# Attention into two layered products on one core: the softmax sums divided earlier, a start in written order, a new order of the parts, and six more filled slots

## The chip, the cores and the metric

The kernel runs on one core of one Trainium2 chip. The metric is device time in microseconds (us), the median of three runs. The core has a TensorE (PE) for products, VectorE (DVE), ScalarE (ACT) and GpSimd (POOL) for the rest, and SyncE (SP), whose queue issues all transfers of this kernel. PEld is the load of weights into TensorE.

## The reference

q, k and v have 4 batches, 8 heads, 576 rows and 64 columns, f one value per row; all is float32 (weights are handed to the kernel as float64 words).

```
scores = q k^T / 8 ;  cum = cumsum(log(clip(f, 1e-4, 1)))
scores = where(causal, scores + cum_i - cum_j, -1e9)
attn   = exp(scores - rowmax);  attn = attn / (rowsum(attn) + 1e-9)
x = attn v               -> 2304 x 512
h = x w_in               -> 2304 x 2048;  g = h tanh(log(1 + e^h)) (Mish);  y = g w_out   -> 2304 x 512
ab = (y w1) * (y w2)     -> 2304 x 1024;  out = (ab w3) w_out2                            -> 2304 x 512
```

## The kernel before

**Two phases.** Phase A has the attention, the conversion of the float64 words of all weights, the product w3 w_out2 ("wp"), and as much of the first layer as is ready. Phase B has the rest of the first layer and then two halves ("quads") of the later layers. A float32 operand stands as a high and a low part, and one product is three passes (high high, high low, low high). In phase B seven products of half matrices stand for eight; they are numbered 1 to 7, and the letter o is that number.

**Slots.** The 32 heads go in 16 pairs, each pair in four slots (64, and four for what is left). Slot j of a pair has the scores of query blocks c = (0, 1), (2, 3), (4) for j = 0, 1, 2 (`score`, L711), the product with v of the pair before at j = 3 (`pv`), and the transposes of the probabilities of the slot before (`turn`, L700). Between them stand products from a list, the filler: 192 of wp in slots 0 to 20, then products of the first layer, 24 in each of the slots 21 to 36, 12 in each of 37 to 52, none in 53 to 63, and 24 in each of 64 and 65 (`plan`, L592). A unit of the first layer is 12 products into one bank, and its copy h goes to DRAM (L554 to L562). Units that are left run in phase B behind the attention (`cover`); there they are 144 products.

**Softmax.** `softmax` takes scores plus mask out of PSUM with a running minimum (VectorE, L390, L396, L397), then exponentials on ScalarE with their row sums (L400). The probabilities stay undivided. At slot 3 of a pair the nine columns of sums get a reciprocal (`inv_sums`, L403), are transposed with the identity (L705), copied (L416), stored in DRAM (L417) and loaded back as a tile R, one row for all partitions of a head (`inv_load`, L419). `x_rows` multiplies the product with v by R (L482).

**The start.** `decay_log` computes log f on 128 partitions of 144 values. `decay_rows` gathers them on 32 partitions of 576 by four transfers (L279), scans them, makes high and low parts of both signs, and loads rows of these into the score operands `aug` (L344 to L348); a copy goes to DRAM for later pairs. Ten weight tiles (two of w3, eight of w_out2) are converted by an exponent pass on ScalarE (L134), three passes on VectorE (L142 to L144), a cast on ScalarE (L99) and a subtraction on GpSimd (L113).

**What sets the order.** TensorE runs in written order. The other engines are ordered at build time by a scheduler from priorities (`high_priority`) and from its own estimate; `issue_after` (`behind`, `between`) keeps an instruction behind another one of its engine.

**The first layer in phase B.** Eight m, seven parts each, 12 products a part, 56 steps. The order is that of `m_order` (L801): 5, 6, 2, 3, 7, then part 1 of the next m, then part 4. Parts 6, 7 and 4 add into the bank of part 1, and the addition to 7 (L1057) must have read that bank before 4 writes it; 5 and 3 share one bank. A hook behind each part puts in `s_sums` and `s_build` for the next m, the conversion of w1 and w2, and at the end `k_begin`, the operands of the next layer. The gate layers use the same `m_layer` and order.

Of the kernel before, what the change touches and what calls it, by code (L numbers as in the profile page):

```python
# [34 lines left out]
LAST = 2 * S - 64  # L35

# [6 lines left out]
NEAR = 2  # L43
MID = 7
EARLY = 10
# [31 lines left out]
class Kernel:  # L77
# [18 lines left out]
    def split(self, raw, hi, lo, hi_eng="act", lo_eng="dve"):  # L96
        nc = self.nc
        if hi_eng == "act":
            nc.scalar.copy(hi, raw)  # L99
# [17 lines left out]
    def cv_load(self, key, src, where=None):  # L117
# [5 lines left out]
        self.nc.sync.dma_start(dst, src)  # L123
# [12 lines left out]
    def cv_bits(self, key):  # L136
# [7 lines left out]
        dve.scalar_tensor_tensor(ti, w[:, :, 0], 29, ti, ALU.logical_shift_right, ALU.bitwise_or)  # L144

    def cv_split(self, key, hi, lo, hi_eng="act", lo_eng="pool"):
        self.split(self.cv.pop(key)[1], hi, lo, hi_eng, lo_eng)
        self.fresh.add(key)
# [45 lines left out]
    def pools(self):  # L194
# [7 lines left out]
        self.inv_scr = d.tile([NPAIR, 9, 128], F32, name="inv_scr")  # L202
# [14 lines left out]
    def att_pool(self):  # L217
# [12 lines left out]
        self.ident = a.tile([128, 128], F32, name="ident")  # L230
        self.m1 = a.tile([128, 512], BF16, name="m1")
# [39 lines left out]
    def decay_rows(self, between, after):  # L271

        nc, dve = self.nc, self.nc.vector
        lf = self.att.tile([128, S], F32, name="lf", tag="xx", bufs=1)
        cum = self.att.tile([128, S], F32, name="cum", tag="R", bufs=1)
        for i in range(4):
            ins = nc.sync.dma_start(lf[0:32, 144 * i:144 * i + 144], self.lf[32 * i:32 * i + 32])  # L279
        with self.tc.issue_after(ins.ins):  # L280
            between()
        dve.tensor_tensor_scan(cum[:32], lf[:32], lf[:32], 0.0, ALU.add, ALU.bypass)
        slot = self.pt[0:32, 3].bitcast(F32R)
        ch, cl, nh, nl = [slot[:, i] for i in range(4)]
        dve.tensor_scalar(ch, cum[:32], 8.0, None, ALU.mult)
        nc.scalar.mul(nh, f32(ch), -1.0)
        dve.scalar_tensor_tensor(cl, cum[:32], 8.0, f32(ch), ALU.mult, ALU.subtract)
        dve.tensor_scalar(nl, f32(cl), -1.0, None, ALU.mult)
        cs = self.cum_scr.rearrange("(p t) r c -> t p r c", t=2)
        q, k = f32(slot[:, 0:2]), f32(slot[:, 2:4])  # L290
        self.cum_sb = (q, k)
        self.load_cum(0)
        ins = self.load_cum(1)
        nc.sync.dma_start(cs[0, :, 0:2], q[0:16])
        nc.sync.dma_start(cs[0, :, 2:4], k[0:16])
        nc.sync.dma_start(cs[1, :, 2:4], k[16:32])
        nc.sync.dma_start(cs[1, :, 0:2], q[16:32])
        with self.tc.issue_after(ins.ins):
            after()


    def consts(self):
        nc = self.nc
        make_identity(nc, self.ident)
        nc.gpsimd.memset(self.m1, 0.0)
# [33 lines left out]
    def load_cum(self, h):  # L339
        nc = self.nc  # L340
        t = f32(self.aug[h // 2 % 2])
        r = 64 * (h % 2)
        q, k = (self.cum_scr[h, 0:2], self.cum_scr[h, 2:4]) if h > 1 else [x[16 * h:16 * h + 1] for x in self.cum_sb]
        nc.sync.dma_start(t[r + 2:r + 4, 0:S], k)  # L344
        if h % 2 == 0:
            return nc.sync.dma_start(t[r:r + 2, S:2 * S], q)
        nc.sync.dma_start(t[r:r + 2, 2 * S:KQ], q[..., 512:])
        return nc.sync.dma_start(t[r:r + 2, S:LAST], q[..., :512])  # L348

# [26 lines left out]
    def softmax(self, p, c):  # L376
# [7 lines left out]
        if c < 4:  # L384
# [7 lines left out]
            cols = (c, 5 + c)  # L392
        else:
# [4 lines left out]
            cols = (4,)  # L398
# [4 lines left out]
    def inv_sums(self):  # L403

        nc = self.nc
        r = self.sums[:, 0:9]
        nc.scalar.activation(r, r, AF.Copy, bias=1e-9)
        nc.vector.reciprocal(r, r)
        self.inv = r

    def inv_rows(self, p):

        nc = self.nc
        t = self.att.tile([16, 128], F32, name=f"inv{p}", tag="inv", bufs=1)
        with self.tc.high_priority(offset=HP_SM):
            nc.scalar.copy(t[0:9], self.ps_t[1][0:9, 384:512])  # L416
        nc.sync.dma_start(self.inv_scr[p], t[0:9])  # L417

    def inv_load(self, p):  # L419
        self.R = self.att.tile([128, S], F32, name=f"R{p}", tag="R", bufs=1)  # L420
        d = self.inv_scr[p:p + 1].rearrange("o i q -> o (i q)")
        self.nc.sync.dma_start(self.R[0:64], d[:, :S].broadcast_to([64, S]))
        self.nc.sync.dma_start(self.R[64:128, :512], d[:, 640:].broadcast_to([64, 512]))
        self.nc.sync.dma_start(self.R[64:128, 512:], d[:, S:640].broadcast_to([64, 64]))
# [51 lines left out]
    def x_rows(self, p):  # L476
# [5 lines left out]
        self.nc.vector.tensor_tensor(x, self.ps_v[:, 256:832], self.R, ALU.mult)  # L482
# [59 lines left out]
    def l1_unit(self, b, m, half):  # L542
# [4 lines left out]
        def step(c, k, i):  # L547
# [46 lines left out]
    def plan(self):  # L594
# [8 lines left out]
        cnt += [24] * (L1_S[1] - WP_END) + [12] * 16 + [0] * (NU * NPAIR - L1_S[1] - 16)  # L603
        return cnt + [24, 24] + [0] * NU

    def phase_a(self):
# [12 lines left out]
        self.decay_log()  # L619
        self.load_raw(0)  # L620
        self.consts()
        self.zeros()

# [4 lines left out]
        def after():  # L628
# [677 lines left out]
```

## Time and profile before

| | us |
|---|---|
| median of 3 runs | 958.28 (957.95 to 958.51) |
| the profiled execution | 958.19 |
| its span | 956.4 |
| mean granted TensorE clock | 0.980 |
| TensorE busy | 883.2 (92%) |
| VectorE busy | 687.5 (72%) |
| ScalarE busy | 496.3 (52%) |
| GpSimd busy | 203.4 (21%) |

The span is from the first to the last instruction, and what lies around it is 1.8 us. Busy shares are averages over stages with different limits. A wait is put down to what ended last before it. In the busy table by stretches, PEclk is the granted TensorE clock as a share of full speed.

### The profile page before, as it was taken

Reading aid. Unit: us, or ns where it says so; the run is one execution under the profiler, and the core shown is the slowest. Engines: PE = TensorE matmul, PEld = TensorE weight load, DVE = VectorE, ACT = ScalarE, POOL = GpSimd, SP = SyncE. Lnnn points to the kernel's source line nnn. Section 1 sums busy time; section 2 is a strip of 40 time slices with the busy share of each in tenths; the row PEclk is TensorE's granted clock in tenths of the full one; section 3 lists DMA queues with packets and bytes.
Section 4 is the critical chain, followed back from the end, with each engine's and each line's share of the span. In section 5 each row is a group of like instructions: output and inputs, shape, how many; then the busy total and the mean of one; then the engine's idle time right before and its main releaser. Section 6 shows DMA issues by size and latency. Waiting matters only on the chain.

```text
span 956.4 us, 17581 instructions
## 1 busy us (share of the span) xinstructions
PE 883.2 (92%) x6336; PEld 807.2 (84%) x6336; DVE 687.5 (72%) x1329; ACT 496.3 (52%) x1091; POOL 203.4 (21%) x257
## 2 busy tenths in 40 slices
PE   0699989999998788999989999999999999999998
PEld 0367767888886557999979999999999999999998
DVE  6998788645675685877768889668488797644483
ACT  2566765665675573455544556334395454322152
POOL 4757676413554552000000000000000000000000
PEclk9999999999999989999999999999999999999999
DMA  8457767766777784334335466845977555555552
GB/s 261 146 162 232 241 185 234 238 187 191 232 233 243 246 255 160 120 118 134 113 126 195 156 206 220 291 176 210 399 260 214 170 155 162 169 162 169 156 178 75
DMA packets 129446, 185.99 MB, mean 194 GB/s; under 512 B 12160, under 2 KB 75792, under 8 KB 129360
## 3 DMA queue, kind: packets, MB, share of 16 engines
q1 hardware_dynamic: 129360, 184.88, 59.9%
q8 instruction: 50, 0.82, 0.3%
q14 instruction: 36, 0.29, 0.1%
HBM read 129.33 MB, written 55.42 MB: 193 GB/s over the span
## 4 chain that ended last, share of the span: by engine, by line
PE 72%; DVE 9%; DMA 7%; ACT 4%; issue 4%; POOL 2%; SPq 2%; ACTq 0%; DVEq 0%; POOLq 0%
PE ps_x L970 14%; PE ps_x L1042 14%; PE ps_z L1042 7%; PE ps_y L970 6%; PE ps_z L970 6%; PE ps_l L554 6%; PE ps_s L369 4%; PE ps_y L1042 3%; PE ps_l L520 3%; PE ps_t L437 2%; PE ps_s L471 2%; PE ps_s L373 2%; DMA cvri<-in_w_in_dram 1%; DMA cvru<-in_w_out_dram 1%; DMA ws<-pt 1%
## 5 line engine op out<-in xcount | busy, mean ns | idle before, releaser
L554 PE MATMUL ps_l<-x,wi 128*128 128x288 f32 x624 | 92.6, 303 | 3.2 <-ACT h L561 3.2
L554 PEld LDWEIGHTS ps_l<-x,wi 128*128 128x128 f32 x624 | 85.6, 192 | 10.6 <-issue 5.7
L931 ACT CAST g_h<-y 128x576 fp32r<-128x576 f32 x96 | 63.8, 674 | 57.0 <-PE ps_x L970 25.9
L970 PE MATMUL ps_x<-g_h,ws 128*128 128x288 f32 x512 | 91.0, 296 | 1.2 <-ACT g_h L931 1.0
L932 DVE TENSOR_TENSOR g_l<-y,g_h 128x576 fp32r<-128x576 f32 x96 | 72.1, 754 | 19.2 <-ACT g_h L931 18.3
L400 ACT ACTIVATE P<-P,sum 128x256 f32<-128x256 f32 (+3 forms) x112 | 70.4, 631 | 21.6 <-DVE sum L397 16.1
L970 PEld LDWEIGHTS ps_x<-g_h,ws 128*128 128x128 f32 x512 | 75.6, 188 | 2.1 <-ACT g_h L931 1.5
L369 PE MATMUL ps_s<-raw 64*128 64x128 f32 (+3 forms) x256 | 56.5, 523 | 9.7 <-DMA raw<-in_qk_dram 5.7
L369 PE MATMUL ps_s<-aug 64*128 64x128 f32 (+3 forms) x128 | 39.8, 605 | 21.1 <-DMA aug<-pt 21.1
L390 DVE CUSTOM_DVE_ANT_0 P<-ps_s,m 128x256 f32<-128x256 f32 (+2 forms) x96 | 49.5, 554 | 12.6 <-PE ps_s L369 12.3
L1042 PE MATMUL ps_x<-T,gs 128*128 128x288 f32 x384 | 54.1, 296 | 1.7 <-ACT Cg L1047 0.9
L452 DVE COPY pt<-ps_t 128x128 f32<-128x128 f32 (+1 forms) x64 | 29.6, 483 | 36.1 <-PE ps_t L437 36.1
L970 PE MATMUL ps_x<-g_l,ws 128*128 128x288 f32 x256 | 55.0, 296 | 0.5 <-DVE g_l L932 0.5
L1042 PE MATMUL ps_x<-T,ws 128*128 128x288 f32 x384 | 54.0, 295 | 0.8 <-DVE Cg L1057 0.8
L1042 PEld LDWEIGHTS ps_x<-T,gs 128*128 128x128 f32 x384 | 51.9, 188 | 2.2 <-ACT Cg L1047 1.1
L1042 PEld LDWEIGHTS ps_x<-T,ws 128*128 128x128 f32 x384 | 52.0, 188 | 1.1 <-DVE Cg L1057 1.1
L931 ACT CAST h_h<-ab 128x576 fp32r<-128x576 f32 x48 | 31.6, 671 | 39.1 <-PE ps_x L970 21.8
L520 PE MATMUL ps_l<-wo,w3h 128*128 128x512 f32 x128 | 45.2, 423 | 5.1 <-POOL wo L113 3.2
L970 PE MATMUL ps_x<-h_h,ws 128*128 128x288 f32 x256 | 46.4, 297 | 0.1
L932 DVE TENSOR_TENSOR h_l<-ab,h_h 128x576 fp32r<-128x576 f32 x48 | 35.9, 755 | 13.6 <-ACT h_h L931 13.4
L471 PE MATMUL ps_s<-pt,va 128*64 128x320 f32 (+3 forms) x384 | 45.0, 383 | 0.0
L437 PE MATMUL ps_t<-ident,P 128*128 128x128 f32 x288 | 40.6, 276 | 2.8 <-DVE pt L452 1.9
(271 smaller groups left out, 2274.2 us busy)
## 6 DMA issues: line engine op xcount, KB each, us to landing
ws<-ws SPq DMA_DIRECT2D x112, 512.0 KB
ws<-pt SPq DMA_DIRECT2D x67, 256.0 KB
ws<-gs SPq DMA_DIRECT2D x56, 256.0 KB
h_scr<-h SPq DMA_DIRECT2D x64, 144.0 KB
y<-h_scr SPq DMA_DIRECT2D x16, 576.0 KB
cvrt<-in_w3t_dram SPq DMA_DIRECT2D x16, 512.0 KB
cvri<-in_w_in_dram SPq DMA_DIRECT2D x16, 512.0 KB
cvru<-in_w_out_dram SPq DMA_DIRECT2D x16, 512.0 KB
```

The source lines that it names most:

```text
L369: mm(ps[:, 512 * hh:512 * hh + n], t[r, q0:q0 + 128], t[r, 0:n], start=first, stop=not first)
L390: dve = ttr(P[hh][:, :n], ps[:, 512 * hh:512 * hh + n], self.m1[:, 512 - n:], -0.125, 3.0e38, ALU.add, ALU.min, st[hh])
L400: ins = nc.scalar.activation(t[:, :n], t[:, :n], AF.Exp, bias=b, scale=-1.0, accum_out=self.sums[:, i:i + 1])
L437: tr(self.ps_t[hh][:, o + 128 * k:o + 128 * k + 128], P[:, 128 * k:128 * k + 128], self.ident)
L452: return copy(dst[:, 0:c + 1, 128 * c:128 * c + 128], src)
L471: mm(ps[64 * hh:64 * hh + 64, 256 + q:256 + q + w], lhs, rhs, start=i == 0, stop=i == len(plan) - 1)
L520: mm(o, w, x, start=i == 0, stop=i == 23)
L554: mm(o[:, :TB], w, x, start=i == 0, stop=i == 11)
L931: self.mark(self.nc.scalar.copy(hi, raw))
L932: self.mark(self.nc.vector.tensor_tensor(lo, raw, f32(hi), ALU.subtract))
L970: mm(ps[:, r, :TB], w[:, 256 * a + 128 * e:256 * a + 128 * e + 128], ops[i][b][:, r], start=o in (1, 5, 2) and f == 0 and (a, b) == (0, 0) ...
L1042: mm(bank[:, r, :TB], w[:, i:i + 128], T[o, k][:, b, r], start=o in (1, 2, 5) and (k, a, b) == (0, 0, 0), stop=(k, a, b) == (1, 1, 0), ski ...
```

## The change

- **Start.** The scan runs on 128 partitions of 144 values. A product with a constant matrix `heads` adds up the ends of the earlier quarters of a head, and its column is added to the scan. The parts go to DRAM, and the rows of all heads, the first two included, are loaded from there. ScalarE, VectorE and SyncE follow the written order in this stage; four weight loads stand ahead of the sums and six behind. The subtractions of the ten weight tiles are VectorE's. The first slot's softmax stands behind the fifth tile's conversion (`HOLD`).
- **Division.** R, its transposes and its way through DRAM are gone. `norm` adds 1e-9 to the sums of a slot, takes reciprocals and scales the probabilities in place, one slot later and ahead of that slot's scores: head 0 on ScalarE, head 1 and block 4 on VectorE. `x_rows` is a copy on ScalarE.
- **Filler.** 22 slots hold 12 first-layer products where 16 did; the cover has 72 products where it had 144. Its copies of h run on ScalarE where they ran on VectorE.
- **Buffers.** The weight builds rotate through six places where they had five.
- **Order of the parts.** Part 5 of the next m stands between its part 1 and this m's part 4; in the last m part 7 stands ahead of 3. The hooks of `s_sums`, `s_build`, the w1 and w2 conversions and `k_begin` move to other parts.

```diff
+HOLD = 4
-NEAR = 2
-MID = 7
-EARLY = 10
+NEAR = 4
...
     def decay_rows(self, between, after):
-        lf = self.att.tile([128, S], F32, name="lf", tag="xx", bufs=1)
-        cum = self.att.tile([128, S], F32, name="cum", tag="R", bufs=1)
+        two = [self.x_tile(f"cu{i}", F32) for i in range(2)]
+        cum, c8 = two[0][:, 0:144], two[0][:, 144:288]
+        offs = two[0][:, 288:289]
+        slot = two[1].bitcast(F32R).rearrange("p (r c) -> p r c", r=4)
+        dve.tensor_tensor_scan(cum, self.lf, self.lf, 0.0, ALU.add, ALU.bypass)
+        nc.tensor.matmul(self.ps_l[0][:, 0:1], self.heads, cum[:, 143:144], start=True, stop=True)
+        between()
+        dve.tensor_copy(offs, self.ps_l[0][:, 0:1])
+        dve.tensor_scalar(c8, cum, offs, 8.0, ALU.add, ALU.mult)
+        ch, cl, nh, nl = [slot[:, i] for i in range(4)]
+        dve.tensor_copy(ch, c8)
+        nc.scalar.mul(nh, f32(ch), -1.0)
+        dve.tensor_tensor(cl, c8, f32(ch), ALU.subtract)
+        dve.tensor_scalar(nl, f32(cl), -1.0, None, ALU.mult)
         for i in range(4):
-            ins = nc.sync.dma_start(lf[0:32, 144 * i:144 * i + 144], self.lf[32 * i:32 * i + 32])
...
+            nc.sync.dma_start(self.cum_scr[:, :, 144 * i:144 * i + 144], f32(slot[32 * i:32 * i + 32]))
+        after()
         self.load_cum(0)
+        self.load_cum(1)
...
-    def inv_sums(self): ...
-    def inv_rows(self, p): ...
-    def inv_load(self, p): ...
+    def norm(self, p, cs):
+        dve = self.nc.vector
+        a = 2 * cs[0]
+        r = self.sums[:, a:a + 2 * len(cs) - (cs == (4,))]
+        dve.tensor_scalar(r, r, 1e-9, None, ALU.add)
+        dve.reciprocal(r, r)
+        for c in cs:
+            n = min(128 * (c + 1), S)
+            for hh in range(1 if c == 4 else 2):
+                P = self.P[c][hh][:, :n]
+                r = self.sums[:, 2 * c + hh:2 * c + hh + 1]
+                if hh or c == 4:
+                    dve.tensor_scalar(P, P, r, None, ALU.mult)
+                else:
+                    self.nc.scalar.activation(P, P, AF.Copy, scale=r)
...
-        self.nc.vector.tensor_tensor(x, self.ps_v[:, 256:832], self.R, ALU.mult)
+        self.nc.scalar.copy(x, self.ps_v[:, 256:832])
...
-                    if self.late_l1:
-                        self.nc.vector.tensor_copy(t, o[:, :TB])
-                    else:
-                        self.nc.scalar.copy(t, o[:, :TB])
+                    self.nc.scalar.copy(t, o[:, :TB])
...
-        cnt += [24] * (L1_S[1] - WP_END) + [12] * 16 + [0] * (NU * NPAIR - L1_S[1] - 16)
+        cnt += [24] * (L1_S[1] - WP_END) + [12] * 22 + [0] * (NU * NPAIR - L1_S[1] - 22)
...
+        self.consts()
+        self.lo_eng = "dve"
+        with self.tc.manual_schedule(engines={getattr(mybir.EngineType, e) for e in ("Activation", "DVE", "SP")}):
+            self.zeros()
+            self.decay_log()
+            self.load_raw(0)
+            early(0, NEAR)
+            self.decay_rows(lambda: go(0), lambda: early(NEAR, NEAR + 1))
+            early(NEAR + 1, len(first))
+            for i in range(1, len(first)):
+                go(i)
+                if i == HOLD:
+                    self.hold = self.last
+                fin(i - 1)
+            fin(9)
+        self.lo_eng = "pool"
...
+            if live and j:
+                with self.tc.high_priority(offset=HP_SM):
+                    self.norm(p, ((0, 1), (2, 3), (4,))[j - 1])
             if live and j < 3:
                 score(p, ((0, 1), (2, 3), (4,))[j])
...
     def m_order(n):
-        seq = [(0, 1)]
+        seq = [(0, 1), (0, 5)]
         for m in range(n):
-            seq += [(m, o) for o in ORDER_M[1:-1]]
             if m + 1 < n:
-                seq.append((m + 1, 1))
+                seq += [(m, o) for o in (6, 2, 3, 7)] + [(m + 1, 1), (m + 1, 5)]
+            else:
+                seq += [(m, o) for o in (6, 2, 7, 3)]
             seq.append((m, 4))
...
-            g = self.nbs % 5
+            g = self.nbs % 6
...
-                st = self.att.tile([128, 512], F32R, name=f"bs{l}_{u}_{o}", tag="bs", bufs=1)
+                st = self.att.tile([128, 512], F32R, name=f"bs{l}_{u}_{o}", tag="bs", bufs=2)
...
-                    if o == 2:
+                    if o == 6:
                         self.s_sums(m + 1)
+                    elif o == 2:
+                        self.s_build(m + 1, 0)
                     elif o == 3:
-                        self.s_build(m + 1, 0)
-                    elif o == 7:
                         self.s_build(m + 1, 1)
-            elif o == 5:
+            elif o == 6:
                 self.begun = self.k_begin("g0_", 8, self.y)
...
-            if o == 1 and m and f <= 16:
+            if o == 7 and m and f <= 16:
                 with self.between():
                     self.v_convert(f - 2)
-            if o == 2 and f < 16:
+            if o == 7 and f < 16:
                 self.v_load(f)
...
-            if o == 6 and m and f <= 16:
+            if o == 4 and m and f <= 16:
                 with self.between():
                     self.v_convert(f - 1)
```

## Rows read from the trace of the kernel before

**Rows 1.** Busy table by stretches: stretch and length, engines, PEclk, DMA share, GB/s.
```profile
0.00:47.60 47.60, 16.01 (x49) 9.88 (x50) 37.94 (x72) 20.31 (x41) 27.99 (x49) 0.96 0.67 205
47.60:321.30 273.70, 261.36 (x1814) 209.20 (x1814) 191.82 (x473) 177.26 (x527) 150.01 (x180) 0.98 0.71 218
321.30:373.60 52.30, 43.25 (x300) 30.64 (x298) 34.63 (x93) 30.23 (x96) 25.37 (x29) 0.87 0.74 239
377.26:398.64 21.38, 20.82 (x145) 20.61 (x145) 21.34 (x53) 10.63 (x24) 0.00 (x0) 0.92 0.18 63
398.64:499.37 100.73, 93.05 (x674) 90.94 (x675) 75.90 (x152) 52.44 (x85) 0.00 (x0) 0.98 0.37 122
```

**Rows 2.** Chain that ended last, first layer and gate layer: start us, us, what.
```profile
433.67 1.86 PE ps_x L1042 x12
...
445.64 1.86 PE ps_x L1042 x12
...
609.92 4.77 PE ps_x L1042 x36
...
621.04 4.77 PE ps_x L1042 x36
```

**Rows 3.** Chain that ended last, the start.
```profile
28.02 2.25 DMA cum_scr<-pt
...
53.90 2.58 PE ps_l L520 x10
```

**Rows 4.** Timeline of POOL, the start: start us, us, line, op.
```profile
46.86 1.59 POOL L113 TENSOR_TENSOR wo<-cvo,wo 128x256 fp32r<-128x256 f32 x2 [0.19 <-ACT wo L99]
```

**Rows 5.** Waits of PE, 44 to 380 us: total us, times, longest.
```profile
PE ps_t L441 <- ACT pt L452: 9.6, 5, 3.4
PE ps_s L369 <- DVE xr L482: 3.8, 2, 2.8
PE ps_z L554 <- DVE xr L482: 3.6, 1, 3.6
```

**Rows 6.** Waits of SP's queue, 264 to 378 us.
```profile
SPq L422 <- DMA inv_scr<-inv: 14.6, 6, 4.1
```

**Rows 7.** Waits, 398 to 500 us.
```profile
PE ps_x L1042 <- DVE Cx L1057: 4.4, 7, 0.8
...
PE ps_z L1042 <- ACT sp L1111: 1.7, 1, 1.7
...
PE ps_z L1042 <- DVE sp L1112: 1.6, 1, 1.6
```

**Rows 8.** Timeline of DVE, the start.
```profile
13.67 0.31 DVE L268 SCALAR_TENSOR_TENSOR lg<-lg,lg 128x144 f32<-128x144 f32 x1
...
24.99 0.69 DVE L143 SCALAR_TENSOR_TENSOR cvo<-cvro,cvo 128x512 int32<-128x512 int32 x1
...
31.41 1.21 DVE L143 SCALAR_TENSOR_TENSOR cvt<-cvrt,cvt 128x512 int32<-128x512 int32 x1
```

**Rows 9.** Chain that ended last, one transpose of the sums (16 in all).
```profile
318.32 0.11 PE ps_t L705
```

**Rows 10.** Groups of DVE by form, 48 to 145 us: count, busy us, mean ns, idle before.
```profile
L142 DVE TENSOR_SCALAR cvt<-cvt 128x512 int32<-128x512 int32 x13 | 7.0, 535 | 0.0
...
L482 DVE TENSOR_TENSOR xx<-ps_s,R 128x576 f32<-128x576 f32 x4 | 3.0, 745 | 0.0
...
L408 DVE RECIPROCAL sum<-sum 128x9 f32<-128x9 f32 x5 | 1.0, 201 | 0.0
```

**Rows 11.** Groups of ACT by form, 264 to 375 us.
```profile
L134 ACT ACTIVATE cvu<-cvru 128x512 f32<-128x512 f32 x10 | 6.6, 674 | 0.6 <-POOL bs L850 0.4
```

**Rows 12.** Chain that ended last, the cover's first products.
```profile
377.26 2.68 PE ps_z L554 x12
```

**Rows 13.** Timeline of DVE, the last copy of the cover.
```profile
400.88 0.45 DVE L559 COPY h<-ps_y 128x288 f32<-128x288 f32 x1
```

**Rows 14.** Waits of PE, 500 to 956 us.
```profile
PE ps_x L1042 <- DVE Cg L1057: 1.7, 2, 0.8
```

More of the change, by code (lines that the diff above doesn't have):

```diff
@@ L98, in split @@
         if hi_eng == "act":
-            nc.scalar.copy(hi, raw)
+            self.last_act = nc.scalar.copy(hi, raw)
         else:
@@ L143, in cv_bits, with cv_split @@
         dve.scalar_tensor_tensor(ti, w[:, :, 1], SIGN, ti, ALU.bitwise_and, ALU.bitwise_or)
-        dve.scalar_tensor_tensor(ti, w[:, :, 0], 29, ti, ALU.logical_shift_right, ALU.bitwise_or)
-    def cv_split(self, key, hi, lo, hi_eng="act", lo_eng="pool"):
-        self.split(self.cv.pop(key)[1], hi, lo, hi_eng, lo_eng)
+        return dve.scalar_tensor_tensor(ti, w[:, :, 0], 29, ti, ALU.logical_shift_right, ALU.bitwise_or)
+    def cv_split(self, key, hi, lo):
+        self.split(self.cv.pop(key)[1], hi, lo, "act", self.lo_eng)
         self.fresh.add(key)
@@ L304, in consts @@
         make_identity(nc, self.ident)
+        nc.gpsimd.memset(self.heads, 0.0)
+        for i in range(1, 4):
+            nc.gpsimd.affine_select(self.heads, self.heads, [[-1, 128]], ALU.not_equal, 1.0, base=32 * i,
+                                    channel_multiplier=1)
         nc.gpsimd.memset(self.m1, 0.0)
@@ L339, in load_cum @@
     def load_cum(self, h):
-        nc = self.nc
+        dma = self.nc.sync.dma_start
         t = f32(self.aug[h // 2 % 2])
         r = 64 * (h % 2)
-        q, k = (self.cum_scr[h, 0:2], self.cum_scr[h, 2:4]) if h > 1 else [x[16 * h:16 * h + 1] for x in self.cum_sb]
-        nc.sync.dma_start(t[r + 2:r + 4, 0:S], k)
+        i = 16 * (h % 2) + h // 2
+        q, k = self.cum_scr[i, 0:2], self.cum_scr[i, 2:4]
+        dma(t[r + 2:r + 4, 0:S], k)
         if h % 2 == 0:
-            return nc.sync.dma_start(t[r:r + 2, S:2 * S], q)
-        nc.sync.dma_start(t[r:r + 2, 2 * S:KQ], q[..., 512:])
-        return nc.sync.dma_start(t[r:r + 2, S:LAST], q[..., :512])
+            dma(t[r:r + 2, S:2 * S], q)
+            return
+        dma(t[r:r + 2, 2 * S:KQ], q[..., 512:])
+        dma(t[r:r + 2, S:LAST], q[..., :512])
     def load_v(self, p):
@@ L391, in softmax @@
                           ALU.min, st[hh])
-            cols = (c, 5 + c)
+            cols = (2 * c, 2 * c + 1)
         else:
@@ L401, in softmax @@
         return ins, dve
[L403 to L424, printed above, removed]
+    def norm(self, p, cs):
[13 more added lines that the diff above has]
+                    self.nc.scalar.activation(P, P, AF.Copy, scale=r)
     @staticmethod
@@ L626, in early, with fin @@
                 self.cv_load(first[i][0], first[i][1], where[i])
-        def after():
-            early(MID, EARLY)
-            self.load_v(0)
-        early(0, NEAR)
-        self.decay_rows(lambda: early(NEAR, MID), after)
-        def go(i):
-            key, _, fin, *a = first[i]
-            self.cv_exp(key)
-            self.cv_bits(key)
-            fin(*a)
-            if i + EARLY < len(first):
-                self.cv_load(first[i + EARLY][0], first[i + EARLY][1], where[i + EARLY])
-        for i in range(10):
-            go(i)
+        def go(i):
+            self.cv_exp(first[i][0])
+            self.last = self.cv_bits(first[i][0])
+        def fin(i):
+            first[i][2](*first[i][3:])
+        self.consts()
[14 more added lines that the diff above has]
+        self.lo_eng = "pool"
+        self.go_act, self.go_sp = self.last_act, self.last_sp
         misc, conv = {}, {}
@@ L679, in phase_a @@
             s = NU * p
[L680 to L683 removed]
+            at(s + 1 if p else 0, self.load_v, p)
             if p + 1 < NPAIR:
@@ L703, in turn @@
                     self.transposes(p, c)
-                if cs == (4,):
-                    self.nc.tensor.transpose(self.ps_t[1][0:9, 384:512], self.inv, self.ident)
-                    self.inv_rows(p)
                 for c in cs:
@@ L714, in score @@
                     self.scores(p, c)
-                for c in cs:
-                    self.act, self.dve = self.softmax(p, c)
+                with self.behind(None if self.slot else self.hold):
+                    for c in cs:
+                        self.act, self.dve = self.softmax(p, c)
         for s in range(NU * (NPAIR + 1)):
@@ L727, in slots @@
             with self.tc.high_priority(offset=HP_SM):
-                for key in conv.get(s, []):
-                    self.cv_exp(key)
+                with self.behind(self.go_act if s < 3 else None):
+                    for key in conv.get(s, []):
+                        self.cv_exp(key)
+            if live and j:
+                with self.tc.high_priority(offset=HP_SM):
+                    self.norm(p, ((0, 1), (2, 3), (4,))[j - 1])
             if live and j < 3:
@@ L746, in slots @@
             with self.behind(self.act):
-                for fn, a in misc.get(s, []):
-                    fn(*a)
+                with self.behind(self.go_sp if s < 2 else None):
+                    for fn, a in misc.get(s, []):
+                        fn(*a)
             self.run_filler(n - k)
@@ L1216, in hook @@
         def hook(m, o):
-            if m == 7 and o == 5:
+            if m == 7 and o == 6:
                 self.begun = self.k_begin(f"h{q}_", 4, ab)
```

33 lines of the change are left out of this document (3 added, 30 removed).

## The prediction

> **What bounds the kernel now.** I began with the busy table of the page and then cut the span at the joints of the program [rows 1]. The reader is to see that TensorE is nearly full in most stretches and that what is lost lies in a few. From 0 to 47.6 us it works 16.0 us. From 47.6 to 321.3 (the attention with many filler products) it lacks 12.3 us. From 321.3 to 373.6 (the end of the attention) it lacks 9.1 us, and its granted clock is 0.87 of full, which is a further 0.13 x 52.3 = 6.8 us at most. The 21.4 us from 377.3 are the cover, in which VectorE is busy for 21.34. From 398.6 to 499.4 stands the first layer, 56 steps of 12 products; three steps that nothing delays take 4.77 us [rows 2], so one takes 1.59, a product 0.1325, and of the 100.7 us 89.2 are work and 11.5 are lost. Behind 499.4 the page has TensorE at 97 to 99%, and the change touches little there.
>
> Next I read the chain that ended last and the view of waits. In the start the chain goes from one conversion to the next; the first ten-product run of the next W3 tile starts at 53.90 [rows 3], and the last of the first eight output weights is ready at 48.45, by a GpSimd subtraction [rows 4]. In the attention TensorE waits for ScalarE's copies of transposes (9.6 us) and for the product with R (3.8 us), and at its end 3.6 us more for R [rows 5]. SyncE's queue stands 14.6 us in six pairs until the stored inverse sums have landed [rows 6]; every other transfer stands behind it. In the first layer TensorE waits seven times for VectorE's addition to part 7, and once each for the two halves of a built weight, the last one [rows 7]. The first of these shows as a period of 11.97 us per m against 11.12 in the gate layer with the same seven steps [rows 2].
>
> All sums stand against the profiled execution, 958.19 us with a span of 956.4; that is 0.09 below the median of the three timed runs (958.28).
>
> **1. The start.** The gather of the log rows (four transfers and the wait behind them) goes; the scan runs on 128 partitions over 144 columns, a one-column product adds the offsets, and the sums take two trips through DRAM in place of one. Such a trip took 2.25 us [rows 3]. With the log chain no longer interleaved with two conversions and their wait it ends at about 9.7 instead of 14.0 [rows 8]; a quarter of the scan (0.4), one conversion (three instructions, together 1.8) and five small operations (0.2 each) put the store at 13.4, its landing at 18, that of the loads at 22. Some lateness here costs nothing, since the first softmax is held behind the fifth conversion (13.0 + 4 x 1.8 + 3 x 0.62 = 22.1). VectorE then carries all the rest: nine conversions x 1.8 = 16.2, ten subtractions that GpSimd did, some 0.62 each (a two-input pass over 512 columns, as L143 undisturbed, 0.69, less the overlap with the next) = 6.2, and softmaxes and copies of slots 0 to 2, some 5.5. 13.0 + 27.9 = 41 for the last output weight against 48.45; the next W3 tile follows with 1.8 on VectorE, 0.6 on ScalarE and two GpSimd pieces, at 46 against 53.90. I take **-7**, with -4 (weights land late, ScalarE between) and -9.5 as ends. It is no loss that work moves to the busier engine: L143 took 0.69 us alone and 1.21 while GpSimd subtracted [rows 8], and the move takes the slow form away.
>
> **2. Normalisation.** It removes 16 transposes of the sums, 0.11 us each on the path [rows 9]: -1.8. ScalarE's copy of the rows, SyncE's four issues per pair and their blocking wait go too. VectorE loses the product with R (0.745) and one reciprocal (0.2), and gets per pair three additions and three reciprocals of a few columns (0.2 each, by L408) and five scalings of 128 to 576 columns (0.535 for 512 by L142, so 2.0 in all): net +2.3 us [rows 10]. ScalarE gets four scalings and the copy of x, by 0.674 us for 512 columns [rows 11] some 2.6 us. VectorE is at 191.8 / 273.7 = 0.70 in the long stretch and goes to about 0.82, ScalarE from 0.65 to 0.78. The scalings are new waits in both queues: behind them stand the next slot's exponentials, the copies of transposes and the h copies, and TensorE's transposes wait for these. In slots with 9 to 24 products between scores and transposes I let the products hide them, and the long stretch (47.6 to 321.3) gets **0** with term 3's first slot: bounds +12 (a quarter of a microsecond at each of 48 turns) and -8 where the free queue shortens ScalarE's waits. A scaling by a per-partition column is not in the trace; L142 (a constant, 0.535) and L482 (a second tensor, 0.745 for 576) bound it, and I take the first, which has one input as it has.
>
> The page SBUF — State Buffer of the Trainium skill, section "SBUF: two separate sides", says that a VectorE operation in a two-port mode and a GpSimd operation lock each other out for the whole instruction. By that rule each of the 80 scalings on VectorE could stand behind one whole GpSimd piece, 80 x 0.8 = 64 us of queue [rows 4]; L142's mean of 0.535 was measured while GpSimd worked in 150 of 273.7 us [rows 1] and holds its share of such waits already, so by the rows nothing is added, and I go by these.
>
> **3. Six slots with 12 products.** One of them (slot 53) ends before 321.3 and costs 1.6, which the transposes' -1.8 cancels. The other 60 products add 60 x 0.1325 = 8.0 to the 52.3 us. Against it: both waits for R's product (-3.8); some of the five waits for ScalarE's copies, two of which lie here (-1.5); and, since filled slots have no gap in which the clock falls, about half of the 6.8 us of missing clock (-3). For it: in slots 59 to 63 nothing covers the scaling, at three of their turns 1.15 us each (addition and reciprocal 0.4, scaling 0.55, hand-overs 0.2) = +3.5. Sum **+3**, ends -3 and +8.
>
> **4. End of the attention and cover.** The last product with R was waited for 3.6 us; a ScalarE copy of 576 columns replaces it, 0.9 with the hand-over: -2.7. 72 products fewer: 72 x 0.1325 = -9.5. The cover's first twelve took 2.68 us [rows 12] in place of 1.59 after that gap; half of the difference back, -0.5. **-12.7**, ends -9 and -13.5. The end at -9: ScalarE now also has the h copies of the cover, and one that waits for its buffer's transfer stands in front of the x copy.
>
> **5. First layer.** Part (m+1, 5) now stands between parts 7 and 4, so the addition to 7 has 3.2 us in place of 1.6; seven losses of 0.85 go (-5.9). The last weight's wait (1.6 + 1.7) goes for the most part, its sums starting one step earlier, and some clock with it (-3.5). But behind the shorter cover VectorE is late: it needs 24 us from the end of the attention to the last L559 copy [rows 13], 4.4 less without these twelve copies, then 0.7 for one addition and some 3.4 for the next weight's sums and halves (two 512- and four 256-wide sums and one subtraction, at 0.69 for 512): 23.7. TensorE asks for that weight after 1.0 + 9.5 + 7 x 1.59 = 21.6: +2.1, or +2.4 with the hand-over. Sum **-7**, ends -2 and -10.
>
> **6. Gate layers.** The order 7, 3, 4 at their ends takes away two waits of 0.85 [rows 14]: **-1.6**, ends -2 and 0. The k layers keep their steps.
>
> -7 + 0 + 3 - 12.7 - 7 - 1.6 = -25.3: 958.2 - 25.3 = **933 us**.
>
> **The rivals.** (a) The attention gives it back: VectorE and ScalarE at 0.8 in an order fixed at build time, a quarter of a microsecond lost at each of 48 turns, 12 us: 945. For it speaks that TensorE already waits 9.6 us for ScalarE's copies; against it that the filler stands there. (b) More comes free: SyncE's 14.6 us in six pairs and the sixth build buffer shorten the transfers for which ScalarE's builds, and behind them the copies, wait, and the clock stays up: 12 us more, 921. Against it: the weights' own transfers keep their size. (c) In the first layer VectorE's order stays late and only the cover is won; term 5 is 0: 940. (d) The other side: the scalings are exposed at every turn. Addition, reciprocal, scaling and hand-over are 1.15 us at 48 turns, 55 in full; from 0.53 us per turn on the 25.3 are gone, and at 0.6 the time is 962. The means would be scalings held by GpSimd, as L143 was. Against it: 59 of the 64 slots hold 1.6 to 3.2 us of products. (e) That the cover is not shorter, because first-layer products find no weights ready in the six slots: 72 x 0.1325 = 9.5 come back, 942; their weights are split by slot 30, so this has no chance of its own.
>
> **How the numbers follow.** Forecast 0.55 (924 to 942), (a) 0.14 (941 to 950), (b) 0.18 (914 to 924), (c) 0.07, (d) 0.06, of which 0.01 lies within 0.2%, about what a measurement can tell from no change. Leaving out (d) and the outer parts of (a) and (b) gives 921 to 946. Faster 0.94, same 0.01, slower 0.05.
>
> **What would show it.** The next W3 tile's first products at 46 to 49 us (1). No wait of SyncE for stored sums, and TensorE late for scalings only in slots 59 to 63 (2, 3). The cover's first product 1 us behind the attention's last, and 72 of them (4). A wait of 2 us before the second weight of the first layer, and a period near 11.2 (5). It would be wrong if the attention's period per pair rose by more than half a microsecond beyond the added products.

## The result, and the profile after

The changed kernel takes 932.59 us (929.24 to 936.2, four runs) where the kernel before took 958.39 (957.95 to 960.77): a ratio of 0.9727 [0.9682, 0.9771]. The forecast was 933 (921 to 946). The profiled execution is 929.24 with a span of 927.5, against 958.19 and 956.4.

Busy table by stretches of the kernel after, cut at the same joints as [rows 1]: the first scores of block 4 (pair 0), those of pair 13 (slot 54), the last product with v, the cover's first product, and the first layer's first step. Columns as there.

```profile
0.00:39.53 39.53, 15.59 (x51) 10.33 (x52) 36.80 (x90) 19.60 (x42) 9.82 (x33) 0.91 0.75 226
39.53:310.62 271.09, 260.02 (x1814) 209.20 (x1814) 222.78 (x589) 205.34 (x566) 152.12 (x179) 0.98 0.68 212
310.62:369.63 59.01, 48.97 (x357) 37.93 (x355) 42.46 (x116) 38.89 (x109) 24.65 (x29) 0.94 0.61 201
370.35:380.15 9.80, 9.80 (x74) 9.80 (x75) 9.80 (x25) 6.17 (x15) 0.00 (x0) 1.00 0.20 71
380.15:472.45 92.30, 89.60 (x674) 89.12 (x674) 80.45 (x164) 57.12 (x101) 0.00 (x0) 1.00 0.41 132
```

Set against [rows 1], the length of each stretch gives the whole difference of the spans. The last column has the same for a second profiled execution of the same kernel (932.09 us, a span of 930.3):

| stretch | before | after | difference | term forecast | difference, second execution |
|---|---|---|---|---|---|
| start | 47.60 | 39.53 | -8.1 | -7 | -8.1 |
| attention to pair 13 | 273.70 | 271.09 | -2.6 | 0 | +1.2 |
| end of the attention | 52.30 | 59.01 | +6.7 | +3 | +4.7 |
| gap and cover | 25.04 | 10.52 | -14.5 | -12.7 | -14.5 |
| first layer | 100.73 | 92.30 | -8.4 | -7 | -8.4 |
| the rest | 457.0 | 455.05 | -2.0 | -1.6 | -1.0 |
| sum | 956.4 | 927.5 | -28.9 | -25.3 | -26.1 |

The two stretches of the attention move by 2 to 4 us from one execution to the next; the others hold. They are in the second execution:

```profile
39.54:314.41 274.87, 262.06 (x1813) 210.06 (x1813) 222.64 (x589) 205.57 (x566) 151.98 (x179) 0.97 0.68 208
314.41:371.42 57.01, 47.38 (x357) 37.06 (x355) 41.90 (x116) 38.76 (x110) 24.46 (x29) 0.97 0.62 209
```

In the first layer TensorE is busy for 89.60 of 92.30 us, so that little is left there. The one stretch that became longer is the end of the attention. Waits of TensorE in the attention of the kernel after (36 to 372 us; total, times, longest):

```profile
PE ps_t L428 <- ACT P L415: 12.0, 6, 4.1
PE ps_l L545 <- ACT h L549: 2.5, 2, 1.9
PE ps_t L428 <- ACT pt L415: 2.0, 1, 2.0
PE ps_l L511 <- POOL w3l L112: 2.0, 2, 1.8
```

The waits for R [rows 5] are gone, and those for ScalarE's copies are 0.6 in place of 9.6. Their place has been taken by waits of the transposes for the scalings on ScalarE (L415), 14.0 us in seven. Timeline of TensorE at the attention's end, the four longest of them:

```profile
315.12 0.87 PE L428 MATMUL ps_t<-ident,P 128*128 128x128 f32 x6 [1.52 <-ACT P L415]
...
333.88 0.87 PE L428 MATMUL ps_t<-ident,P 128*128 128x128 f32 x6 [1.52 <-ACT P L415]
...
345.79 0.44 PE L428 MATMUL ps_t<-ident,pt 128*128 128x128 f32 x2 [2.01 <-ACT pt L415]
...
353.57 1.54 PE L428 MATMUL ps_t<-ident,P 128*128 128x128 f32 x6 [4.10 <-ACT P L415]
```

They are 9.15 us together. The first two stand in slots 54 and 58, which hold 12 products each, the other two in slots 61 and 62, which hold none. What stood in front of the last is in the chain that ended last, from the scores of block 4 on, and beside it in GpSimd's timeline:

```profile
347.08 2.42 PE ps_s L370 x6
...
349.98 1.09 DVE cvv L143
351.08 0.61 DVE sum L405
351.68 0.42 DVE P L394
...
352.25 0.58 issue
352.83 0.19 ACT P L397
353.01 0.52 ACT P L415
353.53 0.04 issue
353.57 1.54 PE ps_t L428 x6
```

```profile
349.80 0.72 POOL L841 TENSOR_TENSOR pt<-cvu,pt 128x256 fp32r<-128x256 f32 x1 [6.86 <-ACT pt L840]
350.49 2.75 POOL L841 TENSOR_TENSOR pt<-pt 128x256 fp32r<-128x256 f32 x3
354.50 1.41 POOL L841 TENSOR_TENSOR bs<-cvu,bs 128x256 fp32r<-128x256 f32 x2 [1.26 <-ACT bs L840]
```

The scaling of blocks 2 and 3 stands in ScalarE's queue behind the exponential of block 4 (352.14, 0.78 us), which waits for a softmax half on VectorE, which stands behind a conversion's pass and the addition to the sums. By VectorE's timeline the pass takes 1.18 us there and the four-column addition 0.68, both beside GpSimd's pieces of 349.80 to 353.24; seven us earlier, with GpSimd idle but for its first 0.06 us, they take 0.68 (342.89) and 0.15 (343.49).

### The profile page after: what moved, and what is told of

Read it like the earlier page. It is cut to its first block, busy times and chain, and to the rows that moved or that the text cites. A ratio compares the mean times of both kernels' runs of the same rounds, so it can differ in the third digit from the quotient of the medians.

```text
span 927.5 us, 17664 instructions
## 1 busy us (share of the span) xinstructions
PE 872.5 (94%) x6322; PEld 802.6 (87%) x6322; DVE 720.5 (78%) x1473; ACT 534.2 (58%) x1151; POOL 186.6 (20%) x241
## 4 chain that ended last, share of the span: by engine, by line
PE 69%; DVE 10%; ACT 5%; DMA 3%; issue 3%; POOL 2%; SPq 0%; ACTq 0%; POOLq 0%; DVEq 0%
PE ps_x L1033 16%; PE ps_x L961 15%; PE ps_z L1033 8%; PE ps_z L961 6%; PE ps_y L961 6%; PE ps_l L545 6%; PE ps_y L1033 4%; PE ps_s L462 3%; ACT P L397 2%; PE ps_t L428 2%; PE ps_s L366 2%; DVE P L413 1%; DVE P L387 1%; DMA cvri<-in_w_in_dram 1%; PE ps_s L370 1%
## 5 line engine op out<-in xcount | busy, mean ns | idle before, releaser
L545 PE MATMUL ps_l<-x,wi 128*128 128x288 f32 x696 | 103.8, 303 | 2.5 <-ACT h L549 2.5
L545 PEld LDWEIGHTS ps_l<-x,wi 128*128 128x128 f32 x696 | 95.5, 191 | 10.9 <-issue 6.1
L397 ACT ACTIVATE P<-P,sum 128x256 f32<-128x256 f32 (+3 forms) x112 | 70.4, 630 | 13.4 <-DVE sum L387 9.7
L366 PE MATMUL ps_s<-raw 64*128 64x128 f32 (+3 forms) x256 | 49.8, 470 | 5.7 <-DMA raw<-in_qk_dram 5.4
L428 PEld LDWEIGHTS ps_t<-ident,P 128*128 128x128 f32 x288 | 33.9, 144 | 16.2 <-ACT P L415 15.2
L462 PE MATMUL ps_s<-pt,va 128*64 128x320 f32 (+3 forms) x384 | 47.5, 399 | 0.0
L923 DVE TENSOR_TENSOR h_l<-ab,h_h 128x576 fp32r<-128x576 f32 x48 | 35.8, 754 | 14.7 <-ACT h_h L922 14.6
L1038 ACT COPY Cg<-ps_x 128x576 f32<-128x576 f32 x16 | 10.2, 640 | 63.0 <-PE ps_x L1033 62.9
```

What stands on the lines that cost most here:

```text
L366: mm(ps[:, 512 * hh:512 * hh + n], t[r, q0:q0 + 128], t[r, 0:n], start=first, stop=not first)
L397: ins = nc.scalar.activation(t[:, :n], t[:, :n], AF.Exp, bias=b, scale=-1.0, accum_out=self.sums[:, i:i + 1])
L428: tr(self.ps_t[hh][:, o + 128 * k:o + 128 * k + 128], P[:, 128 * k:128 * k + 128], self.ident)
L462: mm(ps[64 * hh:64 * hh + 64, 256 + q:256 + q + w], lhs, rhs, start=i == 0, stop=i == len(plan) - 1)
L545: mm(o[:, :TB], w, x, start=i == 0, stop=i == 11)
L923: self.mark(self.nc.vector.tensor_tensor(lo, raw, f32(hi), ALU.subtract))
```

## Experiments

Ratios are to the kernel before, timed on the same chip. Diffs are against the kernel after unless said otherwise. An edit can shift its line numbers by one or two.

**The kernel after once more.**

> The changed kernel once more, as the measure for the runs beside it. Its four runs so far lie between 929.2 and 936.2. Theory: 932 with the same spread of some 0.7%. Rival (the spread was chance): within 0.3% of one value.

931.72 us (929.16 to 936.09), 0.9723 [0.9698, 0.9747]: the same value and spread, as the theory had it. A difference of more than some 3 us to this one is taken as one below.

**The six slots taken back.**

```diff
-        cnt += [24] * (L1_S[1] - WP_END) + [12] * 22 + [0] * (NU * NPAIR - L1_S[1] - 22)
+        cnt += [24] * (L1_S[1] - WP_END) + [12] * 16 + [0] * (NU * NPAIR - L1_S[1] - 16)
```

> The changed kernel with 16 instead of 22 slots of 12 products, the cover at 144 again. Theory: the attention ends 5 us sooner (9.6 us of products, of which 4.6 lay in gaps and low clock), the cover is 9.5 longer, and the first layer's 2.4 us wait for ScalarE goes: 2 to 3 us slower than the changed kernel. Rival: the slots' gaps are latency that products do not fill; then the attention ends 9 us sooner and the time is the same or 2 us less.

942.06 us, 0.9835 [0.9813, 0.9856]: 10.3 slower, and both theories missed. The cover is longer by 9.4 us (19.2 against 9.8), as it must be; but the attention's end did not become shorter. Busy table of its last stretch, pair 13 to the last product with v, and one of its waits:

```profile
311.40:373.34 61.94, 44.76 (x295) 31.68 (x295) 42.79 (x116) 37.07 (x105) 25.14 (x29) 0.86 0.54 179
```

```profile
336.40 1.54 PE L428 MATMUL ps_t<-ident,P 128*128 128x128 f32 x6 [6.69 <-ACT P L415]
```

It has 62 instructions of TensorE fewer than the kernel after (295 against 357) and lasts 2.9 us longer. The waits for scalings grew from 14.0 to 21.7 us, and the granted clock of the stretch is 0.86 where it was 0.94. Five other traces with the six slots and the scalings in place (the second execution, the order, the start, the five buffers and the block-wise scalings below) have 56.9 to 60.4 us for this stretch. So with the scalings in place, the way from scores to scaled probabilities sets this stretch: the products in it lie in time that would be lost without them, and the clock is higher with them. The first layer took 89.8 us, without the wait of 2.3 told below; that is the slots' price.

**The six slots alone, in the kernel before** (the line above, 16 to 22).

> The kernel of before with the six more slots alone (cover 72). Theory: the gaps of its last pairs take the products as they do in the changed kernel, the cover is 9.5 shorter, and VectorE, which has the h copies there, is late for the first layer by 3 to 5: 5 us faster than before. Rival: without scaling waits the last pairs have too few gaps; 1 us faster or the same.

959.17 us, 1.0000 [0.9979, 1.0021]: the rival was right. The attention's end is 5.9 us later (379.56 against 373.68; 4.5 of it behind pair 13, for 8.0 us of products) and the first layer 4 longer (104.65 against 100.6), which eats the shorter cover. SyncE still stands 15.7 us for the stored sums [rows 6], and one copy of a transpose is 5.06 late behind a ScalarE cast that waited 5.93 for its buffer's transfer. The same edit is worth 10 us in one kernel and nothing in the other. The two kernels differ in the division, the order of the parts and the engine of the cover's copies of h; which of these decides was not separated.

**The order of the parts and the hooks taken back.**

```diff
-        seq = [(0, 1), (0, 5)]
+        seq = [(0, 1)]
         for m in range(n):
+            seq += [(m, o) for o in ORDER_M[1:-1]]
             if m + 1 < n:
-                seq += [(m, o) for o in (6, 2, 3, 7)] + [(m + 1, 1), (m + 1, 5)]
-            else:
-                seq += [(m, o) for o in (6, 2, 7, 3)]
+                seq.append((m + 1, 1))
...
```

> The changed kernel with the order of the parts and the hooks of before. Theory: the period per m in the first layer is 11.97 us again instead of 11.15, the last weight is late by 3.5, and the gate layers lose 1.6: 8 us slower. Rival: behind the shorter cover VectorE is the limit anyway, whatever the order; then 3 us slower.

945.18 us, 0.9861 [0.9837, 0.9885]: 13.5 slower, where 8 was the theory. The first layer takes 105.1 us against 92.3. Waits of TensorE in it:

```profile
PE ps_x L1032 <- DVE Cx L1047: 4.2, 7, 0.8
PE ps_x L1032 <- ACT Cx L1037: 2.3, 1, 2.3
PE ps_z L1032 <- ACT sp L1101: 1.8, 1, 1.8
PE ps_z L1032 <- DVE sp L1102: 1.2, 1, 1.2
```

The first, third and fourth are those of [rows 7]. They sum to 7.2; the second stands in the kernel after too. The granted clock of the stretch is 0.95 where the kernel after has 1.00, which is most of the rest (0.05 x 105 = 5 us).

**The order alone, in the kernel before.**

> The kernel of before with the new order of the parts and the hooks alone. Theory: the first layer goes from 100.6 to 91 us (seven losses of 0.82, the last weight's wait), the gate layers lose 1.6 less, and behind the cover of 144 nothing is late at its start: 10 to 11 us faster than before, 0.989. Rival: with the h copies on VectorE its queue is too full; 5 us faster.

946.71 us, 0.9867 [0.9847, 0.9887]: 960 x 0.0133 = 12.8 faster, of which the first layer has 10.7 and the gate layers 1.1 each. Its first layer in the busy table:

```profile
398.30:488.20 89.90, 89.46 (x672) 89.22 (x673) 74.06 (x148) 51.40 (x84) 0.00 (x0) 1.00 0.43 138
```

Behind the long cover nothing is late in it, and the seven short waits are gone with the clock's loss. Of the parts that were tried alone or taken back alone, the order is worth most, and its gain is the same within the noise with the rest and without.

**The start taken back** (decay log on 32 rows, GpSimd's subtractions, no written order; some 90 lines).

```diff
-        dve.tensor_tensor_scan(cum, self.lf, self.lf, 0.0, ALU.add, ALU.bypass)
-        nc.tensor.matmul(self.ps_l[0][:, 0:1], self.heads, cum[:, 143:144], start=True, stop=True)
...
+        for i in range(4):
+            ins = nc.sync.dma_start(lf[0:32, 144 * i:144 * i + 144], self.lf[32 * i:32 * i + 32])
...
```

> The changed kernel with the start of before: gather and scan on 32 partitions, GpSimd's subtractions, the order left to the scheduler. Theory: its first slot 2 stands at 47 to 48 us instead of 39.5 and the shift lasts: 7 to 8 us slower than the changed kernel (932). Rival: the weights' transfers in the next pairs are the limit, so the lead is lost there; 0 to 3 us slower.

938.05 us, 0.9772 [0.9751, 0.9794]: (0.9772 - 0.9723) x 959 = 4.7 slower, by the two intervals anywhere from 1.5 to 8. At pair 0 its trace is 6.9 late (46.39 against 39.53), and at the last product with v, which ends at 377.48, it is 6.1 behind the second execution of the kernel after (371.42) and 7.9 behind the first (369.61). So the traces show the lead kept as far as the cover; whether some of it is lost, as 4.7 would have it, the times don't decide.

**The division behind the product with v again** (R, its way through DRAM and five buffers; slots, start, order as after).

```diff
-            if live and j:
-                with self.tc.high_priority(offset=HP_SM):
-                    self.norm(p, ((0, 1), (2, 3), (4,))[j - 1])
...
+            at(s + 3, self.inv_sums)
+            at(s + 5, self.inv_load, p)
```

> The changed kernel with the division behind the product with v (R, its transposes, its way through DRAM) and, since R needs the room, five build buffers. Theory: TensorE loses its 12 to 14 us of waits for scalings, but the products with R, SyncE's wait and the transposes come back, in the last pairs with 3.6 us at the very end: 3 to 6 us slower. Rival: dividing early costs more than it gives, as 61.9 us from pair 13 to the end with 16 slots against 52.3 before suggest; then 3 to 6 us faster.

939.19 us, 0.9772 [0.9748, 0.9796]: 4.7 slower, within the theory's 3 to 6, though the intervals allow 1 to 8. The last product with v ends at 374.32 against 369.61, the gap in front of the cover is 2.1 against 0.7, and a 6.24 us wait for a copy of a transpose is back.

**Five build buffers** (`% 5`, one place less).

> The changed kernel with five build buffers. Theory: ScalarE's waits of 5 to 7 us for a build's transfer, seen with R in the last pairs, come from SyncE's queue, which stands for the stored sums; without R five buffers do: within 1 us of the changed kernel (0.972 of before). Rival: the sixth buffer took them away; then one wait of 4 to 6 us comes back, 0.977.

932.33 us, 0.9709 [0.9691, 0.9727]: the same. The sixth place is worth nothing.

**The scalings block by block.**

```diff
-                    self.norm(p, ((0, 1), (2, 3), (4,))[j - 1])
+                    for c in ((0, 1), (2, 3), (4,))[j - 1]:
+                        self.norm(p, (c,))
```

> The changed kernel with sums, reciprocal and scaling taken block by block instead of two blocks together. Theory: TensorE's waits for ScalarE's scaling (14 us over nine turns) are for the most part a wait of block 2 for block 3's exponentials; they halve, 3 to 5 us faster. Rival: the waits are ScalarE's and VectorE's queues, and four more small operations of 0.2 us per pair come in; same or 2 us slower.

938.25 us, 0.9794 [0.9776, 0.9812]: 6.5 slower. The waits for L415 fell from 14.0 to 4.1 us, as meant, but those for ScalarE's copies of transposes (0.6 to 5.1) and of h (2.5 to 6.8) grew: the waits moved, and did not go. The three together are 16.0 where they were 17.1, so they don't explain the 6.5 by themselves; the trace has block 4 of pair 0 at 41.39 (39.53 in the kernel after) and 278.6 us from there to pair 13 (271.1 and 274.9). Why, stays open.

**Products from behind the last scalings into their slots.** Slot 64's 24 products go to slots 61 and 62 (first line), or all 48 of slots 64 and 65 to slots 59 to 62 (second).

```diff
+        cnt[61] = cnt[62] = 12
+        return cnt + [0, 24] + [0] * NU
...
+        cnt[59:63] = [12] * 4
+        return cnt + [0, 0] + [0] * NU
```

> The changed kernel with the 24 products of slot 64 in slots 61 and 62, 12 each. Theory: the waits for scalings there (2.0 and 4.1 us) are filled and the clock stays up, nothing waits in slot 64: 3 to 5 us faster than the changed kernel. Rival: the wait moves to slot 64, where nothing then stands between the last scores and their transposes; the same.

> The changed kernel with the 48 products of slots 64 and 65 in slots 59 to 62, 12 each. Theory: two of these slots have no wait to fill and slot 65 loses what covers the last copies in front of the last product with v: 1 to 3 us slower than with slot 64 alone moved (0.9665), about 0.969. Rival: every product that leaves the end is gained; 0.964.

The first: 928.22 us, 0.9665 [0.9643, 0.9687], 5.6 faster, against the theory's 3 to 5. The second: **922.85 us** (921.65 to 925.68), 0.9616 [0.9596, 0.9636]. The theory, which left slots 64 and 65 something to hide, was wrong and the rival right. It is the fastest kernel of the study. Its waits for scalings are 8.6 us where they were 14.0, and the end of the attention has the same 357 instructions of TensorE as the kernel after, at full clock, in 50.57 us where that took 59.01:

```profile
310.95:361.52 50.57, 46.00 (x357) 36.15 (x355) 42.23 (x116) 38.17 (x110) 25.17 (x29) 1.00 0.72 236
```

**The first layer's casts behind the copies.** On the first of these two, ScalarE's casts of the operands for parts 3, 7 and 4 are held to their place between the parts.

```diff
-                self.x_operands(T, ({1: 3, 5: 7, 6: 4}[o],))
+                with self.between():
+                    self.x_operands(T, ({1: 3, 5: 7, 6: 4}[o],))
```

> The changed kernel with slot 64's products in slots 61 and 62, and in the first layer the casts for parts 3, 7 and 4 kept behind the copy of the part before. Theory: the wait of 2.3 us of part 6 for ScalarE's copy, which stands behind eight casts, goes: 2 us faster than with the move alone, 0.9645. Rival: the casts then come too late for part 3; the same.

928.99 us, 0.9676 [0.9660, 0.9691], against 0.9665 without: the same, the rival right. The wait at part 6 is gone, and the wait at the second weight, five steps later, has grown in its place. The first layer takes 97.8 us against 94.2 without the edit. Timelines of TensorE: the kernel after, then the kernel without the edit, then with it.

```profile
385.57 1.84 PE L1033 MATMUL ps_x<-TX,sp 128*128 128x288 f32 x12 [2.26 <-ACT Cx L1038]
```

```profile
379.02 1.85 PE L1034 MATMUL ps_x<-TX,sp 128*128 128x288 f32 x12 [2.26 <-ACT Cx L1039]
...
387.85 0.80 PE L1034 MATMUL ps_z<-TX,sp 128*128 128x288 f32 x4 [0.60 <-ACT sp L1103]
389.40 1.32 PE L1034 MATMUL ps_z<-TX,sp 128*128 128x288 f32 x8 [0.76 <-DVE sp L1104]
```

```profile
392.19 0.91 PE L1034 MATMUL ps_z<-TX,sp 128*128 128x288 f32 x4 [4.08 <-ACT sp L1103]
393.68 2.29 PE L1034 MATMUL ps_z<-TX,sp 128*128 128x288 f32 x8 [0.58 <-DVE sp L1104]
```

## Why the prediction was right, and where it was not

**The sum.** 933 against 932.59 is closer than the terms were. In the profiled execution, at 929.24 the fastest of the four, term 3 is 3.7 us worse than forecast and the other five together 7.3 us better; that they cancel in half, and that the median lies 3.4 above this execution, is luck.

**1, start: right, a little short.** The scores moved by 8.1, the next W3 tile's first product with its low part stands at 46.68 against the 46 to 49 named. Two waits of TensorE for output weights (2.67 and 1.84, L102) fall ahead of 39.53. The sum takes for granted that a lead is kept to the end; the start taken back shows it kept as far as the cover, and its time (4.7 for 6.9) leaves open whether all of it is.

**2, the long stretch: right in time, wrong in one reason.** VectorE is at 222.78 / 271.09 = 0.82 and ScalarE at 0.76, as worked out. The scalings do not take 2.0 us per pair, though. Groups of VectorE by form in the kernel after, 40 to 310 us, and then 0 to 40 us (count, busy us, mean ns, idle before):

```profile
L413 DVE TENSOR_SCALAR P<-P,sum 128x576 f32<-128x576 f32 x13 | 11.9, 913 | 0.2
L413 DVE TENSOR_SCALAR P<-P,sum 128x512 f32<-128x512 f32 x12 | 9.6, 798 | 0.0
L413 DVE TENSOR_SCALAR P<-P,sum 128x256 f32<-128x256 f32 x13 | 9.0, 690 | 0.0
L413 DVE TENSOR_SCALAR pt<-pt,sum 128x128 f32<-128x128 f32 x13 | 8.6, 664 | 0.2
L413 DVE TENSOR_SCALAR P<-P,sum 128x384 f32<-128x384 f32 x12 | 6.7, 558 | 0.1
```

```profile
L413 DVE TENSOR_SCALAR P<-P,sum 128x512 f32<-128x512 f32 x1 | 0.5, 481 | 0.0
L413 DVE TENSOR_SCALAR P<-P,sum 128x384 f32<-128x384 f32 x1 | 0.4, 415 | 0.0
L413 DVE TENSOR_SCALAR P<-P,sum 128x256 f32<-128x256 f32 x1 | 0.3, 348 | 0.0
L413 DVE TENSOR_SCALAR pt<-pt,sum 128x128 f32<-128x128 f32 x1 | 0.3, 282 | 0.0
```

One pair is 3.6 us by the first five. Undisturbed it is 2.05: the last four, and 0.52 for 576 columns at 353.82 in the last pair, between two GpSimd pieces. The slow ones stand where GpSimd works, the quick ones where it does not: from 11.1 to 45.9 us it does nothing. In the long stretch itself ten of the 63 lie clear of every GpSimd piece; they take 0.28 to 0.48 us, each the undisturbed time of its form. That is shown by their places; no experiment took GpSimd's work away. The page SBUF — State Buffer of the Trainium skill, section "SBUF: two separate sides", has the rule for it, and the prediction set it aside because L142's mean was thought to hold its share of such waits. It held little: L142's 0.535 is 0.42 undisturbed (the same pass, L141 in the new start), 0.12 of waiting, where the scalings have 20 / 63 = 0.32 each. The rule's direction was right; its full price, a piece of 0.8 at each of these 63 scalings, 50 us, was not paid, 20 were. The term came out at -2.6 all the same (+1.2 in the second execution), since the products hide nearly all turns of that stretch: 4.9 us of its waits are scalings, in three (104.60, 126.80 and 278.99).

**3, the six slots: the step that was wrong, +6.7 for +3 (+4.7 in the second execution).** The item at fault is the scaling exposed in slots 59 to 63, three turns of 1.15, +3.5. It measured 6.1 us in two turns (slots 61 and 62), and 3.0 more came in slots 54 and 58, whose 12 products the forecast let hide it. With the three of the long stretch, five of the seven waits stand in filled slots, and the sign "TensorE late for scalings only in slots 59 to 63" did not hold. The 1.15 us per turn counted only the turn's own four instructions, not what the built order puts ahead of them (an exponential, a softmax half, a conversion's pass), nor the GpSimd pieces beside it. The missing clock came back as put, (1 - 0.94) x 59.0 = 3.5 against 6.8. And "60 x 0.1325 = 8.0" was no cost here: the slots taken back show the stretch no shorter. In this stretch products and scalings should not have been added but compared, the longer chain setting the time.

**4, cover: right.** The gap is 0.74 where 0.9 was put for a copy of x. The 72 products gave 9.5 as put; the slow clock of the old cover's first three runs (6.37 us in place of 4.77, of which 0.5 was counted) and 0.56 us of idle time at its end went as well.

**5, first layer: right in size, in another place.** A wait of 2.26 stands against the 2.1 to 2.4 forecast, but five steps earlier, at part 6, and for ScalarE: its copy of part 1 (384.89) stands behind eight casts of operands (382.22, 2.76 us). The place forecast, the second weight, lies behind it: where the first wait was taken away, TensorE stood there for 4.08 and 0.58, and for 0.60 and 0.76 in the same kernel with that wait; the rest came with the edit. In the kernel after ScalarE's half of a weight stands 4.3 us for VectorE's sum (392.37), though TensorE does not wait for it. The size was in part luck: the 24 us of the working run from the cover's first product (377.26) to the end of the last copy (401.33), though it says from the end of the attention, while the 21.6 on TensorE's side begin there, with a gap of 1.0. From one origin the wait would have been forecast at 3.1. The period is 11.14 (11.2 forecast), and the last weight's wait is gone.

**6, gate layers: right.** 1.8 us in the two; with the order alone, 1.1 each.

**The rivals.** (a) did not come: the scalings cost 14.0 us of waits, but they replace 13.4 of the old kind (9.6 and 3.8). (b) did not come: SyncE's queue stands as long as before, 14.1 us in eight for copies of h (L550) in place of 14.6 for the stored sums, the sixth buffer gave nothing, and the clock came back by about what the forecast had counted. (c) fell: the order's gain holds behind the short cover. (d) fell: 14.0 us over 48 turns is 0.29 a turn, with 0.53 as its point, and where the products were taken from the slots the waits grew at once. (e) fell: the cover has its 72 products.

## What to carry to other kernels

Filler products are free only where another chain sets the time, so first find which one does: here the same six slots gained nothing in one kernel and 10 us in the other, and moving 48 products from behind the last waits into their slots gave 10 more ((0.9723 - 0.9616) x 959). Before pricing an added instruction, list what the built order puts ahead of it on its engine, and use a duration measured beside the engines that will be busy then. When a wait is taken away, look at the one that stands behind it: twice here (part 6, the block-wise scalings) others grew by about as much.

## What the runs showed of the hardware

The runs of the kernel after lie between 929 and 936, those of the kernel before between 955 and 966. Two profiled executions of the kernel after (929.24 and 932.09) part at 64 us, where TensorE waits for GpSimd's half of a W3 tile. Busy table of the first from 59 to 80 us, and its timeline of TensorE:

```profile
59.00:80.00 21.00, 19.18 (x120) 13.97 (x119) 18.53 (x45) 16.30 (x43) 17.90 (x21) 1.00 0.61 192
```

```profile
63.97 0.51 PE L511 MATMUL ps_l<-wo,w3l 128*128 128x512 f32 x1 [1.82 <-POOL w3l L112]
...
65.29 2.81 PE L462 MATMUL ps_s<-pt,va 128*64 128x256 f32 x24
```

The same of the second:

```profile
59.00:80.00 21.00, 18.45 (x102) 13.05 (x100) 17.27 (x44) 16.12 (x43) 15.04 (x17) 0.84 0.59 173
```

```profile
65.49 0.80 PE L511 MATMUL ps_l<-wo,w3l 128*128 128x512 f32 x1 [2.32 <-POOL w3l L112]
...
67.92 4.68 PE L462 MATMUL ps_s<-pt,va 128*64 128x256 f32 x24
```

The wait is 2.32 us in place of 1.82. Behind it the granted clock of the stretch is 0.84 where the other stays at 1.00, 24 products with v take 4.68 in place of 2.81, and the pair 25.2 in place of 21.3. Half a microsecond went in and four came out. Seven more traces, of kernels with the same start, have this wait. Where it is 0.71, 0.75, 1.02 or 1.65 us (the casts behind the copies, five buffers, slot 64's products moved, the old order), the clock of the stretch is 1.00; where it is 2.32, 2.32 or 2.34 (six slots back, 48 products moved, block-wise scalings), it is 0.92, 0.92 and 0.84. So in all nine the lower clock goes with the longer wait, but no run changed this wait alone, and other waits differ beside it (the block-wise scalings have one of 1.48 in front). It does not set the whole time either: the kernel with 922.85 us, the fastest, is one of those with 2.32, and the one with five buffers, with 0.75, took 932.07 in its profiled execution.
